# Retention and two gated products on one core: the first block's second group becomes the last group of the first product

## The chip, the core and the metric

One Trainium2 chip, one of its cores. The metric is device time in microseconds (us) for one execution of the whole program, the median of several runs. In the text PE is TensorE, DVE is VectorE, ACT is ScalarE, POOL is GpSimd and SP is SyncE, which issues the transfers. All arithmetic is fp32, and every matmul operand is a pair of fp32r values, a high and a low piece.

## What is computed

```python
# retention: B, H, S, D = 8, 8, 576, 64
scores = scale * np.matmul(q, k.transpose(0, 1, 3, 2))
Dmat = np.where(rel >= 0, gamma[:, None, None] ** rel[None, :, :], 0.0)
x = np.matmul(scores * Dmat[None], v)          # 4608 tokens x 512 features
# first product and its gate, d_ff = 2048
h = x @ w_in
g = h * np.cos(h)
x = g @ w_out
# second product, d_ff = 768
h = np.maximum(np.maximum(x @ w1, x @ w2), x @ w3)
out = h @ w_out2
```

## The kernel before, in words

The 4608 tokens are nine blocks of 512 columns (`NBLK`). Every large product is made by a Strassen-like scheme with seven products instead of eight: `P_A11, P_S1, P_A12, P_S2, P_S4, P_S3, P_A22` is the order within one group. An operand of a product is a tile `x_x{block}_{product}` with a high piece (ACT, L395) and a low piece (DVE, L399); names in the program's order carry the product's number (0 is A11, 3 is S1, 1 is A12, 4 is S2, 6 is S4, 5 is S3, 2 is A22). A weight pair `w_wi{i}` holds the seven products of two column blocks of `w_in`. It is made from the raw weights: two loads (`first_load`), then `widen` (ACT, L191), `join` (DVE, L196 and L197), `total` (POOL, L203), the four sums (DVE, L210 to L213) and the high and low pieces (ACT; DVE, L236 and L232). `lead_in` spreads these over steps by a table of eleven numbers.

The program's order is written by hand. A step (`tick`) ends behind each of PE's products; `at(n, fn)` puts work at the n-th step from now, and each engine executes its instructions in that order. The first 17 steps (`LEAD`) hold the attention of units 0 to 7, that is of blocks 0 and 1 (four units a block, two heads each): `att_scores` (PE, L600), `att_mask` (DVE, L609), `att_products` and `att_out` (PE, L631, L667, L679), `att_decay` (DVE, L695). Then come the groups of the first half of `x @ w_in`, stage A: for each block j two groups, `a{j}_0` with weight pairs `wi0` and `wi1` and `a{j}_1` with `wi2` and `wi3`. A group is seven steps, but the last product (A22) is made in the midst of the next group, so the very first group has six. `group_in` copies or adds the results (ACT L469; DVE L475), and `gate_half` spreads the gate (ACT L526 and L536, DVE L530 and L539) and its store. Between the products stand the attention units of the later blocks (`start_of(n)`, one each 11/3 steps), the building of the operands of block j (`build_in`, due at step 14 j, its differences L391 on POOL except for the last block), their stores to HBM (L792) and, once a block, the making of a further weight pair (`background`). Behind stage A come `in_unit` (the other half of `x @ w_in`, with operands `y` loaded back from HBM by `load_operands`), the product with `w_out`, and the second product; nothing of these is changed but the line numbers.

```python
for i, n in ((2, 10), (3, 13)):          # raw weights of pairs wi2, wi3
at(13, lambda: lead_in(2, 0, nc.vector, nc.vector, SPREAD))
at(16, lambda: lead_in(3, 0, nc.vector, nc.vector, SPREAD))
SPREAD = (0, 1, 2, 1, 2, 3, 5, 4, 5, 6, 7)
```

With this table the first low pieces of `wi3` (for A11, A12 and A22) stand at step 21, those for S1 and S2 at step 23; `a0_1` begins at step 23 and its S1 at step 24.

Of the kernel before, what the change touches and what calls it, by code (L numbers as in the profile page):

```python
# [106 lines left out]
def retention_ffn(ctx: ExitStack, tc: tile.TileContext, att, w_in, w_out, w123, w_out2, cst, out):  # L107
# [19 lines left out]
    def f32(t):  # L127
        return t.bitcast(F32)
# [20 lines left out]
    def at(n, fn, turn=LATER):  # L149
        agenda.setdefault(slot[0] + n, [[], [], [], []])[turn].append(fn)  # L150
# [646 lines left out]
    def block_of(j):  # L797
        return quarters_of.setdefault(j, {"name": f"x{j}", "n": NB})
# [8 lines left out]
    for i, n in ((2, 10), (3, 13)):  # L807
        for p in range(2):
            at(n + p, lambda i=i, p=p: first_load(i, p))
    for k, n in enumerate((NLEAD, NLEAD + 1)):  # L810
        at(13 + 3 * k, lambda n=n: att_load(n))
        at(16 + 3 * k, lambda n=n: att_scale(n))
# [5 lines left out]
    at(13, lambda: lead_in(2, 0, nc.vector, nc.vector, SPREAD))  # L818
    at(16, lambda: lead_in(3, 0, nc.vector, nc.vector, SPREAD))
# [5 lines left out]
    def start_of(n):  # L825
        return 3 + (11 * (n - NLEAD)) // 3
# [6 lines left out]
    for j in range(1, NBLK):  # L833
        build_in(block_of(j), per * j, (-11, -4, -3, -1), (-10, -8, -3, -1, 1, 1, 4), xsd[j], nc.vector if j == NBLK - 1 else nc.gpsimd)
    back = [(k, i) for k, n in (("wi", 4), ("wo", 0)) for i in range(n, 8)]
    back += [("b", i) for i in (0, 1, 2, 4, 3, 5, 6, 7, 8)] + [("o", i) for i in range(3)]
    for j in range(NBLK - 2):
        at(per * j + 1, lambda: background(*back.pop(0), True, 3))
    endA = per * NBLK
    for i, n in enumerate((-29, -22, -15, -8)):  # L840
        more = 0
        take_split("wi", 4 + i, endA + n - 2, endA + n + 4, *(endA + n + 5 + more + m for m in (0, 1, 2, 3)))

# [26 lines left out]

    def gate_half(g, half):
        j, k = g["at"]
        q = slice(2 * half, 2 * half + 2)
        dst = gqp[(j - 1) // 2][k][:, q, (j - 1) % 2] if j else gqs[k][:, q]
        steps = {NBLK - 1: (0, 2, 4, 6), NBLK - 2: (0, 1, 3, 4)}.get(j, range(4))
        gate(g[f"s{half}"], f"{g['name']}_{half}", dst, 0 if half else 3, steps)
# [197 lines left out]
    for j in range(NBLK):  # L1074
        for k in range(2):
            group_in(
                [weights["wi", 2 * k + p] for p in range(2)],
                quarters_of[j],
                f"a{j}_{k}",
                gate_half,  # L1080
                (j, k),
                scale=INV2PI,
                seeded=sums_bank,
            )
# [556 lines left out]
```

## Time and profile before

| | |
|---|---|
| median of 3 runs | 1397.74 us (1394.49 to 1398.34) |
| the profiled execution: its time, its span | 1396.51 us, 1394.7 us |
| PE busy | 1363.3 us, 98% of the span |
| DVE busy | 1129.4 us, 81% |
| ACT, POOL busy | 799.0 us (57%), 230.0 us (16%) |
| HBM read, written | 194.28 MB, 137.89 MB |

The profiled execution's own time and its span differ by 1.8 us, which lie around the span. A busy share is a mean over the whole program; what a wait costs is read from the stretch in which it stands. In the timelines a row gives the start in the span, the duration, the engine, the line, the operation with its tiles, the count, and in brackets the idle time before it with what ended it.

### The profile page before, as it was taken

How to read it: one execution, taken by the hardware profiler on the slowest of the kernel's cores; microseconds unless marked ns; L12 is line 12 of the kernel's file. 1: busy time of each engine (PE TensorE's matmuls, PEld its weight loads, DVE VectorE, ACT ScalarE, POOL GpSimd, SP SyncE). 2: the span in 40 equal slices, each digit the busy share in tenths (PEclk: the TensorE clock that was granted, in tenths of full speed). 3: DMA queues.
4: the chain of work that ended last, by engine and by line, in shares of the span. 5: the costliest groups of instructions: out<-in, count | busy, mean ns of one | idle time of the engine just before them, and what ended most of it. 6: DMA issues, size and time to landing. Idle time of an engine off the chain costs nothing.

```text
span 1394.7 us, 22899 instructions
## 1 busy us (share of the span) xinstructions
PE 1363.3 (98%) x8794; PEld 1175.4 (84%) x8794; DVE 1129.4 (81%) x1471; ACT 799.0 (57%) x1238; POOL 230.0 (16%) x259
## 2 busy tenths in 40 slices
PE   7899999999999999999999999999999999999998
PEld 5799999998888887888988888889878888888887
DVE  8988878989687789989879989577777567868884
ACT  6565565568677876666456556444544434444553
POOL 4455555730110000000011110100100000000000
PEclk9999999999999999999999999999999999999999
DMA  9679899988999975664577997343434476255633
GB/s 387 249 286 333 332 343 311 340 314 318 357 349 339 358 286 211 242 226 173 178 258 207 309 255 209 100 154 114 174 134 159 166 273 252 88 180 155 224 106 121
DMA packets 113085, 333.67 MB, mean 239 GB/s; under 512 B 9936, under 2 KB 18256, under 8 KB 107344
## 3 DMA queue, kind: packets, MB, share of 16 engines
q1 hardware_dynamic: 110096, 322.77, 63.9%
q0 software_dynamic: 2880, 9.44, 3.7%
q8 instruction: 69, 1.13, 0.3%
q14 instruction: 40, 0.33, 0.1%
HBM read 194.28 MB, written 137.89 MB: 238 GB/s over the span
## 4 chain that ended last, share of the span: by engine, by line
PE 55%; DMA 5%; DVE 3%; ACT 1%; issue 1%; SPq 0%; ACTq 0%; DVEq 0%
PE d_e L444 12%; PE d_g L976 11%; PE b_g L976 6%; PE b_e L444 6%; PE d_u L1506 5%; PE a_g L976 3%; PE a_e L444 3%; PE b_u L1506 2%; PE d_b L422 2%; PE a_u L1506 1%; DMA mqp<-ext 1%; PE b_b L422 1%; PE d_gs L976 1%; DMA gqp<-s_a 1%; DMA ar_b<-w 1%
## 5 line engine op out<-in xcount | busy, mean ns | idle before, releaser
L976 PE MATMUL d_g<-h_g,w_wo 128*128 128x512 f32 x512 | 157.9, 390 | 0.5 <-ACT o_g L999 0.5
L444 PE MATMUL in<-y,w_wi 128*128 128x512 f32 x672 | 153.0, 389 | 0.0
L444 PEld LDWEIGHTS in<-y,w_wi 128*128 128x128 f32 x672 | 125.9, 188 | 26.5 <-ACT s_a L1112 0.4
L943 DVE TENSOR_TENSOR l_g<-q_g,h_g 128x1024 fp32r<-128x1024 f32 x96 | 116.7, 1229 | 13.9 <-ACT h_g L936 9.5
L469 ACT ACTIVATE ext<-d_e 128x512 f32<-128x512 f32 x72 | 43.1, 599 | 143.1 <-PE d_e L444 143.1
L422 PE MATMUL d_a<-x_x,w_wi 128*128 128x256 f32 x864 | 117.3, 288 | 7.1 <-DVE w_wi L236 4.8
L936 ACT CAST h_g<-q_g 128x1024 fp32r<-128x1024 f32 x96 | 99.0, 1052 | 35.3 <-DVE q_g L927 22.9
L422 PEld LDWEIGHTS d_a<-x_x,w_wi 128*128 128x128 f32 x864 | 107.7, 192 | 12.3 <-DVE w_wi L236 5.0
L976 PEld LDWEIGHTS d_g<-h_g,w_wo 128*128 128x128 f32 x512 | 95.9, 188 | 20.6 <-ACT o_g L999 0.9
L539 DVE SCALAR_TENSOR_TENSOR s_a<-t_a,s_a 128x1024 f32<-128x1024 f32 x68 | 94.1, 1385 | 12.0 <-ACT t_a L536 12.0
L976 PE MATMUL d_g<-l_g,w_wo 128*128 128x512 f32 x256 | 99.8, 390 | 0.2 <-DVE l_g L943 0.2
L530 DVE SCALAR_TENSOR_TENSOR t_a<-s_a,t_a 128x1024 f32<-128x1024 f32 x68 | 88.5, 1303 | 14.2 <-ACT t_a L526 14.2
L526 ACT ACTIVATE t_a<-s_a 128x1024 int32<-128x1024 f32 x68 | 71.9, 1058 | 21.5 <-DVE s_a L1115 15.3
L536 ACT ACTIVATE t_a<-t_a 128x1024 f32<-128x1024 f32 x68 | 72.0, 1059 | 20.5 <-DVE t_a L530 20.2
L444 PE MATMUL d_e<-h_e,w_b 128*128 128x512 f32 x304 | 81.4, 390 | 0.8 <-DVE ext L473 0.8
L976 PE MATMUL b_g<-h_g,w_wo 128*128 128x512 f32 x256 | 79.2, 390 | 1.5 <-ACT h_g L936 1.5
L473 DVE TENSOR_TENSOR ext<-ext,b_e 128x512 f32<-128x512 f32 x36 | 24.7, 686 | 59.4 <-PE b_e L444 51.7
L444 PEld LDWEIGHTS d_e<-h_e,w_b 128*128 128x128 f32 x304 | 56.9, 188 | 12.9 <-DVE ext L473 1.2
L422 PE MATMUL b_a<-x_x,w_wi 128*128 128x256 f32 x432 | 60.6, 290 | 0.9 <-DVE x_x L399 0.9
L976 PEld LDWEIGHTS b_g<-h_g,w_wo 128*128 128x128 f32 x256 | 47.8, 188 | 12.1 <-ACT h_g L936 2.4
L422 PEld LDWEIGHTS b_a<-x_x,w_wi 128*128 128x128 f32 x432 | 55.3, 195 | 3.2 <-DVE x_x L399 1.1
L976 PEld LDWEIGHTS d_g<-l_g,w_wo 128*128 128x128 f32 x256 | 48.1, 188 | 11.0 <-DVE l_g L943 1.0
(371 smaller groups left out, 3322.4 us busy)
## 6 DMA issues: line engine op xcount, KB each, us to landing
u<-att SPq DMA_DIRECT2D x36, 1028.0 KB, 8.3
gqp<-s_a SPq DMA_DIRECT2D x64, 512.0 KB, 6.8
q_g<-gqp SPq DMA_DIRECT2D x64, 512.0 KB, 7.0
xsp<-x_x SPq DMA_DIRECT2D x56, 512.0 KB, 7.5
y<-xsp SPq DMA_DIRECT2D x56, 512.0 KB, 8.8
mqp<-ext SPq DMA_DIRECT2D x24, 512.0 KB, 4.1
st_b<-p_b SPq DMA_DIRECT2D x21, 512.0 KB, 6.4
w_b<-st_b SPq DMA_DIRECT2D x5, 1792.0 KB, 12.8
```

The source lines that it names most:

```text
L422: nc.tensor.matmul(h[:, p * HB : (p + 1) * HB], a, b, start=first and p == 0 and i == 0, stop=i == len(terms) - 1, skip_group_check=True,)
L444: nc.tensor.matmul(dst, a, b, start=first and i == 0, stop=i == len(terms) - 1, skip_group_check=True)
L469: nc.scalar.activation(dst, b[:, :n], AF.Copy, scale=scale)
L473: nc.vector.tensor_tensor(out=dst, in0=dst, in1=b[:, :n], op=ALU.add)
L526: nc.scalar.activation(st["t"], s, AF.Copy, bias=0.25)
L530: nc.vector.scalar_tensor_tensor(out=r, in0=s, scalar=MOST_TURNS, in1=st["t"], op0=ALU.min, op1=ALU.subtract)
L536: nc.scalar.activation(r, r, AF.Sin, scale=TURN, bias=HALF_PI)
L539: nc.vector.scalar_tensor_tensor(out=s, in0=f32(st["t"]), scalar=-1.0, in1=s, op0=ALU.max, op1=ALU.mult)
L936: nc.scalar.copy(h, ts[i][q])
L943: nc.vector.tensor_tensor(out=lo, in0=t, in1=f32(h), op=ALU.subtract)
L976: nc.tensor.matmul(to, a, v[:, p].rearrange("p (b n) -> p b n", b=2) if half and n == 2 else v[:, :, r], start=first and k == 0 and p == 0 ...
L1506: nc.tensor.matmul(dst, a, v, start=first and p == 0 and i == 0 and (wide or mt == 0), stop=p == 2 and i == 2, skip_group_check=True,)
```

## The change

The order of the groups becomes `a0_0, a1_0, a1_1, a2_0, ..., a8_1, a0_1` (`GROUPS`). The group `a0_1` comes last; its seven operand tiles are loaded from HBM (`load_again`, from the copy `xs0` that was stored for a later stage anyway) at the seven steps from 13 before the end of stage A. Weight pairs `wi2` and `wi3` are first needed by `a1_1`; their loads stand seven steps later and their making six. The operands of block 1 are due seven steps earlier, with a table of their own, and so are those of the later blocks. The attention units from 8 on start at once instead of three steps on, one each 7/2 steps, and the loads of units 8 and 9 stand two steps earlier. The background work of a block stands five steps later. The gates of the last three groups are spread, instead of the last two.

```diff
--- before.py
+++ after.py
@@ -804,42 +804,52 @@
     SPREAD = (0, 1, 2, 1, 2, 3, 5, 4, 5, 6, 7)
     for n in range(4, NLEAD):
         at(2 * n - 5, lambda n=n: att_load(n))
-    for i, n in ((2, 10), (3, 13)):
+    for i, n in ((2, 17), (3, 20)):
         for p in range(2):
             at(n + p, lambda i=i, p=p: first_load(i, p))
     for k, n in enumerate((NLEAD, NLEAD + 1)):
-        at(13 + 3 * k, lambda n=n: att_load(n))
-        at(16 + 3 * k, lambda n=n: att_scale(n))
+        at(11 + 3 * k, lambda n=n: att_load(n))
+        at(15 + 3 * k, lambda n=n: att_scale(n))
     lead_in(0, 0, nc.vector, nc.vector, FIRST)
     at(3, claim)
     at(4, lambda: lead_in(1, 0, nc.vector, nc.vector, SECOND))
     for n in range(NLEAD):
         att_unit(n, 2 * n + 1)
-    at(13, lambda: lead_in(2, 0, nc.vector, nc.vector, SPREAD))
-    at(16, lambda: lead_in(3, 0, nc.vector, nc.vector, SPREAD))
+    at(19, lambda: lead_in(2, 0, nc.vector, nc.vector, SPREAD))
+    at(22, lambda: lead_in(3, 0, nc.vector, nc.vector, SPREAD))
     build_in(block_of(0), 0, (10, 14, 15, 16), (10, 12, 14, 16, 17, 18, 19), xsd[0], nc.vector)
     for _ in range(LEAD):
         tick()
 
 
     def start_of(n):
-        return 3 + (11 * (n - NLEAD)) // 3
+        return (7 * (n - NLEAD)) // 2
 
     for n in range(NLEAD, NUNIT):
         if n > NLEAD + 1:
             at(max(0, start_of(n) - 4), lambda n=n: att_load(n))
         att_unit(n, start_of(n))
     per = 14
-    for j in range(1, NBLK):
-        build_in(block_of(j), per * j, (-11, -4, -3, -1), (-10, -8, -3, -1, 1, 1, 4), xsd[j], nc.vector if j == NBLK - 1 else nc.gpsimd)
+    build_in(block_of(1), 7, (-7, -3, -2, -1), (-6, -5, -2, -1, 0, 1, 4), xsd[1], nc.gpsimd)
+    for j in range(2, NBLK):
+        build_in(block_of(j), per * j - 7, (-11, -4, -3, -1), (-10, -8, -3, -1, 1, 1, 4), xsd[j], nc.vector if j == NBLK - 1 else nc.gpsimd)
     back = [(k, i) for k, n in (("wi", 4), ("wo", 0)) for i in range(n, 8)]
     back += [("b", i) for i in (0, 1, 2, 4, 3, 5, 6, 7, 8)] + [("o", i) for i in range(3)]
     for j in range(NBLK - 2):
-        at(per * j + 1, lambda: background(*back.pop(0), True, 3))
+        at(per * j + 6, lambda: background(*back.pop(0), True, 3))
     endA = per * NBLK
     for i, n in enumerate((-29, -22, -15, -8)):
         more = 0
         take_split("wi", 4 + i, endA + n - 2, endA + n + 4, *(endA + n + 5 + more + m for m in (0, 1, 2, 3)))
+
+    again = {}
+
+    def load_again(product):
+        x = again[product] = x4(f"again_{product}", [2, NB], F32R)
+        nc.sync.dma_start(out=f32(x), in_=xss[:, product])
+
+    for r, product in enumerate((P_A11, P_S1, P_A12, P_S2, P_S4, P_S3, P_A22)):
+        at(endA - 13 + r, lambda product=product: load_again(product))
 
     IN_ORDER = (P_A11, P_A12, P_S2, P_S1, P_S3, P_S4, P_A22)
     later_x = {}
@@ -868,11 +878,14 @@
         n = endA + (10, 38, 66, 90)[i]
         take_split("wo", i, n, n + 5, n + 6, n + 7, n + 9, n + 10)
 
+    GROUPS = [(0, 0), *((j, k) for j in range(1, NBLK) for k in range(2)), (0, 1)]
+
     def gate_half(g, half):
         j, k = g["at"]
         q = slice(2 * half, 2 * half + 2)
         dst = gqp[(j - 1) // 2][k][:, q, (j - 1) % 2] if j else gqs[k][:, q]
-        steps = {NBLK - 1: (0, 2, 4, 6), NBLK - 2: (0, 1, 3, 4)}.get(j, range(4))
+        place = GROUPS.index((j, k)) - len(GROUPS)
+        steps = (0, 2, 4, 6) if place >= -3 else (0, 1, 3, 4) if place >= -5 else range(4)
         gate(g[f"s{half}"], f"{g['name']}_{half}", dst, 0 if half else 3, steps)
 
 
@@ -1071,17 +1084,18 @@
             wo_units.append(wo_unit(m, half, base_of[half, m]))
         return base
 
-    for j in range(NBLK):
-        for k in range(2):
-            group_in(
-                [weights["wi", 2 * k + p] for p in range(2)],
-                quarters_of[j],
-                f"a{j}_{k}",
-                gate_half,
-                (j, k),
-                scale=INV2PI,
-                seeded=sums_bank,
-            )
+    for j, k in GROUPS:
+        group_in(
+            [weights["wi", 2 * k + p] for p in range(2)],
+            again if (j, k) == (0, 1) else quarters_of[j],
+            f"a{j}_{k}",
+            gate_half,
+            (j, k),
+            scale=INV2PI,
+            seeded=sums_bank,
+        )
+        if k or not j:
+            quarters_of.pop(j, None)
 
     in_banks = []
```

**PE, between the first group and the next.** `a0_0` is the first group, `x_x1_...` are operands of block 1, `w_wi3` is the last weight pair. Before:

```order
L422 MATMUL b_a0_0_643<-x_x0_6_634,w_wi0_180 128x256 x6
L422 MATMUL b_a0_0_643<-x_x0_6_634,w_wi1_303 128x256 x6
L422 MATMUL d_a0_0_614<-x_x0_5_691,w_wi0_180 128x256 x6
L422 MATMUL d_a0_0_614<-x_x0_5_691,w_wi1_303 128x256 x6
L422 MATMUL d_a0_1_841<-x_x0_0_410,w_wi2_636 128x256 x6
L422 MATMUL d_a0_1_841<-x_x0_0_410,w_wi3_787 128x256 x6
```

Now the group `a1_0` follows, with the weights that are there already:

```order
L422 MATMUL d_a0_0_591<-x_x0_5_678,w_wi0_180 128x256 x6
L422 MATMUL d_a0_0_591<-x_x0_5_678,w_wi1_303 128x256 x6
L631 MATMUL kv9_815<-u2_1_511 64x64 x6
L667 MATMUL po8_822<-u2_0_420 64x128 x8
L679 MATMUL po8_822<-u2_0_420,spare_131 64x128 x2
L679 MATMUL po8_822<-u2_0_420 64x128 x4
L422 MATMUL d_a1_0_849<-x_x1_0_682,w_wi0_180 128x256 x6
L422 MATMUL d_a1_0_849<-x_x1_0_682,w_wi1_303 128x256 x6
L422 MATMUL b_a1_0_884<-x_x1_3_706,w_wi0_180 128x256 x6
L422 MATMUL b_a1_0_884<-x_x1_3_706,w_wi1_303 128x256 x6
```

and `wi2`, `wi3` are read first by `a1_1`, behind it:

```order
L422 MATMUL d_a1_0_849<-x_x1_5_967,w_wi0_180 128x256 x6
L422 MATMUL d_a1_0_849<-x_x1_5_967,w_wi1_303 128x256 x6
L631 MATMUL kv11_1077<-u2_3_869 64x64 x6
L667 MATMUL po10_1084<-u2_2_767 64x128 x8
L679 MATMUL po10_1084<-u2_2_767,spare_131 64x128 x2
L679 MATMUL po10_1084<-u2_2_767 64x128 x4
L422 MATMUL d_a1_1_1109<-x_x1_0_682,w_wi2_875 128x256 x6
L422 MATMUL d_a1_1_1109<-x_x1_0_682,w_wi3_995 128x256 x6
L422 MATMUL b_a1_1_1135<-x_x1_3_706,w_wi2_875 128x256 x6
L422 MATMUL b_a1_1_1135<-x_x1_3_706,w_wi3_995 128x256 x6
```

Between the end of S3 of `a0_0` and the first matmul with `w_wi3` stood six matmuls; now a whole group, two scores and three attention visits stand there.

**DVE, ahead of the last low pieces of `wi3`.** The row `w_wi3...<-s_wi3` makes the low pieces for S1, S2 and S3, S4. Before:

```order
L236 TENSOR_TENSOR w_wi3_787<-fa_wi3_700,w_wi3_787 128x2x256
L232 SCALAR_TENSOR_TENSOR w_wi3_787<-fa_wi3_700,w_wi3_787 128x256
L609 TENSOR_TENSOR u2_0_483<-sc8_0_770,cs_132 128x512
L609 TENSOR_TENSOR u2_0_483<-sc8_1_771,cs_132 128x512
L475 SCALAR_TENSOR_TENSOR s1_a0_0_656<-d_a0_0_614,s1_a0_0_656 128x512
L399 TENSOR_TENSOR x_x1_0_818<-k1_x1_557,x_x1_0_818 128x512
L196 TENSOR_SCALAR ar_wi4_704<-ar_wi4_704 128x512
L197 SCALAR_TENSOR_TENSOR ar_wi4_704<-ar_wi4_704 128x512
L236 TENSOR_TENSOR w_wi3_787<-s_wi3_809,w_wi3_787 128x2x256 x2
```

Now the same piece of the order, which holds the gate of `a0_0` and the additions of `a1_0`:

```order
L236 TENSOR_TENSOR w_wi3_995<-fa_wi3_921,w_wi3_995 128x2x256
L232 SCALAR_TENSOR_TENSOR w_wi3_995<-fa_wi3_921,w_wi3_995 128x256
L196 TENSOR_SCALAR ar_wi4_882<-ar_wi4_882 128x512
L197 SCALAR_TENSOR_TENSOR ar_wi4_882<-ar_wi4_882 128x512
L475 SCALAR_TENSOR_TENSOR s0_a1_0_862<-b_a1_0_884,s0_a1_0_862 128x512
L609 TENSOR_TENSOR u2_3_869<-sc11_0_1013,cs_132 128x512
L609 TENSOR_TENSOR u2_3_869<-sc11_1_1014,cs_132 128x512
L530 SCALAR_TENSOR_TENSOR t_a0_0_1_1038<-s1_a0_0_640,t_a0_0_1_1038 128x1024
L475 SCALAR_TENSOR_TENSOR s1_a1_0_897<-d_a1_0_849,s1_a1_0_897 128x512
L399 TENSOR_TENSOR x_x1_2_1056<-tb_x1_795,x_x1_2_1056 128x512
L399 TENSOR_TENSOR x_x2_0_1058<-k1_x2_864,x_x2_0_1058 128x512
L236 TENSOR_TENSOR w_wi3_995<-s_wi3_1029,w_wi3_995 128x2x256 x2
```

and the rows with which the way there begins, from the addition behind S4 of `a0_0` (L475):

```order
L475 SCALAR_TENSOR_TENSOR s0_a0_0_604<-b_a0_0_627,s0_a0_0_604 128x512
L695 SCALAR_TENSOR_TENSOR k2_x1_697<-po7_731,cs_132 128x64
L695 SCALAR_TENSOR_TENSOR k2_x1_697<-po7_731,cs_132 128x192
L695 SCALAR_TENSOR_TENSOR k2_x1_697<-po7_731,cs_132 128x256
L609 TENSOR_TENSOR u2_1_511<-sc9_0_750,cs_132 128x512
L609 TENSOR_TENSOR u2_1_511<-sc9_1_751,cs_132 128x512
L196 TENSOR_SCALAR t_wi2_708<-t_wi2_708 128x512
L197 SCALAR_TENSOR_TENSOR raw_wi2_1_670<-raw_wi2_1_670,t_wi2_708 128x512
L475 SCALAR_TENSOR_TENSOR s1_a0_0_640<-d_a0_0_591,s1_a0_0_640 128x512
L695 SCALAR_TENSOR_TENSOR k1_x2_864<-po8_822,cs_132 128x128 x2
L695 SCALAR_TENSOR_TENSOR k1_x2_864<-po8_822,cs_132 128x256
L399 TENSOR_TENSOR x_x1_1_843<-k2_x1_697,x_x1_1_843 128x512
```

What moved: the making of `wi2` and `wi3` left the time of block 0's operands and now stands among the operands of block 1, three decays, three masks and the gate of `a0_0`.

**SP, at the end of stage A.** `xsp3<-x_x8...` are stores of the last block's operands, `gqp...<-s` stores of a gate, `y0` the operands of the next stage. Before:

```order
L792 DMA xsp3_75<-x_x8_1_4112 128x2x512
L857 DMA y0_00_4198<-xsp0_72 128x1024
L857 DMA y0_01_4199<-xsp0_72 128x1024
L792 DMA xsp3_75<-x_x8_4_4153 128x2x512
L545 DMA gqp3_0_92<-s1_a7_0_3787 128x2x512
L792 DMA xsp3_75<-x_x8_6_4194 128x2x512
L792 DMA xsp3_75<-x_x8_5_4196 128x2x512
L349 DMA fa_wi7_4261<-wf_wi7_122 128x1024
L857 DMA y0_10_4281<-xsp0_72 128x1024
L857 DMA y0_11_4282<-xsp0_72 128x1024
L545 DMA gqp3_1_93<-s0_a7_1_3995 128x2x512
L792 DMA xsp3_75<-x_x8_2_4256 128x2x512
```

Now the last store of block 8's operands stands ahead, and the loads `again` stand among those of `y0`:

```order
L792 DMA xsp3_75<-x_x8_2_4129 128x2x512
L849 DMA again_0_4207<-xs0_71 128x1024
L867 DMA y0_00_4209<-xsp0_72 128x1024
L867 DMA y0_01_4210<-xsp0_72 128x1024
L849 DMA again_3_4226<-xs0_71 128x1024
L545 DMA gqp3_1_93<-s1_a7_1_3891 128x2x512
L849 DMA again_1_4248<-xs0_71 128x1024
L349 DMA fa_wi7_4268<-wf_wi7_122 128x1024
L849 DMA again_4_4270<-xs0_71 128x1024
L849 DMA again_6_4288<-xs0_71 128x1024
L867 DMA y0_10_4290<-xsp0_72 128x1024
L867 DMA y0_11_4291<-xsp0_72 128x1024
```

## Rows read from the trace of the kernel before

**Rows 1.** Stretches: us; PE, PEld, DVE, ACT, POOL busy; PEclk, DMA share, GB/s

```profile
50.00:60.00 10.00, 3.44 (x25) 2.93 (x24) 9.93 (x21) 4.55 (x10) 4.11 (x4) 0.96 0.57 210
60.00:70.00 10.00, 10.00 (x88) 9.07 (x89) 7.86 (x14) 3.40 (x6) 2.83 (x4) 0.70 0.47 153
```

**Rows 2.** Timeline of PE, from the first group to the second score behind it

```profile
37.23 1.69 PE L422 MATMUL d_a<-x_x,w_wi 128*128 128x256 f32 x12
38.76 1.60 PE L422 MATMUL b_a<-x_x,w_wi 128*128 128x256 f32 x12
...
53.08 1.93 PE L422 MATMUL d_a<-x_x,w_wi 128*128 128x256 f32 x14 [1.77 <-DVE x_x L399]
59.80 1.65 PE L422 MATMUL d_a<-x_x,w_wi 128*128 128x256 f32 x6 [4.79 <-DVE w_wi L236]
61.38 2.08 PE L600 MATMUL sc<-u 64*128 64x128 f32 x16
63.38 2.84 PE L422 MATMUL b_a<-x_x,w_wi 128*128 128x256 f32 x12
...
67.58 0.57 PE L631 MATMUL kv<-u 128*64 128x64 f32 x12
...
69.75 3.13 PE L422 MATMUL d_a<-x_x,w_wi 128*128 128x256 f32 x24
72.81 1.16 PE L600 MATMUL sc<-u 64*128 64x128 f32 x16
```

**Rows 3.** Timeline of DVE, ahead of the last pieces of the fourth weight pair

```profile
37.47 0.84 DVE L391 TENSOR_TENSOR ta_x<-k_x,k_x 128x512 f32<-128x512 f32 x1
...
53.67 2.49 DVE L236 TENSOR_TENSOR w_wi<-s_wi,w_wi 128x512 fp32r<-128x512 f32 x2
...
56.69 0.99 DVE L695 SCALAR_TENSOR_TENSOR k_x<-po,cs 128x64 f32<-128x64 f32 x3
57.60 0.41 DVE L210 TENSOR_TENSOR s_wi<-fa_wi 128x256 f32<-128x256 f32 x1
...
59.06 0.68 DVE L236 TENSOR_TENSOR w_wi<-fa_wi,w_wi 128x512 fp32r<-128x512 f32 x1
...
59.99 1.28 DVE L609 TENSOR_TENSOR u<-sc,cs 128x512 f32<-128x512 f32 x2
61.19 0.68 DVE L475 SCALAR_TENSOR_TENSOR s_a<-d_a,s_a 128x512 f32<-128x512 f32 x1
61.79 0.68 DVE L399 TENSOR_TENSOR x_x<-k_x,x_x 128x512 fp32r<-128x512 f32 x1
62.39 0.42 DVE L196 TENSOR_SCALAR ar_wi<-ar_wi 128x512 uint32<-128x512 uint32 x1
...
63.45 1.28 DVE L236 TENSOR_TENSOR w_wi<-s_wi,w_wi 128x512 fp32r<-128x512 f32 x2
64.66 1.28 DVE L609 TENSOR_TENSOR u<-sc,cs 128x512 f32<-128x512 f32 x2
```

**Rows 4.** Timeline of DVE near the end of stage A, one operation of a gate

```profile
318.00 1.22 DVE L530 SCALAR_TENSOR_TENSOR t_a<-s_a,t_a 128x1024 f32<-128x1024 f32 x1
```

**Rows 5.** Timeline of POOL, one of each kind that the change moves

```profile
51.44 1.04 POOL L203 TENSOR_TENSOR fa_wi<-raw_wi 128x512 uint32<-128x512 uint32 x1 [2.70 <-DVE raw_wi L197]
52.43 0.77 POOL L653 TENSOR_TENSOR u<-u 128x64 f32<-128x64 f32 x1
...
70.59 1.30 POOL L391 TENSOR_TENSOR tb_x<-k_x,ta_x 128x512 f32<-128x512 f32 x1
```

**Rows 6.** Stretch table, the time in which DVE was behind

```profile
35.50:64.10 28.60, 22.04 (x259) 20.28 (x256) 28.36 (x55) 16.23 (x33) 13.85 (x17) 0.91 0.64 254
```

**Rows 7.** What PE waited for from 320 to 345 us

```profile
PE b_a L422 <- DVE x_x L399: 0.9, 1, 0.9
PE d_a L422 <- DVE x_x L399: 0.4, 1, 0.4
```

**Rows 8.** Issues from 318 to 342 us, the last number us to landing

```profile
y<-xsp SPq DMA_DIRECT2D x8, 512.0 KB, 8.8
```

## The prediction

> **What bounds the kernel now.** The page gives PE 98% of the span, so whatever this change brings must come out of the few places where PE waits, or out of new ones. I first read what PE waited for, then the timelines of PE and DVE at these places, then the stretch tables. The change touches stage A alone, and there PE waits twice.
>
> Early, in the first groups: PE is idle 1.77 us ahead of 53.08, for a low piece of an operand, and 4.79 us ahead of 59.80, for the first low piece of `wi3` [rows 2]. Behind these waits it runs slower: the score at 61.38 takes 2.08 us where a later one takes 1.16, S1 at 63.38 takes 2.84 where such a product takes 1.60, and the six matmuls at 59.80 take 1.65, where half a product is about 0.8 [rows 2]. These three are 0.9 + 1.2 + 0.8 = 2.9 us longer. The granted clock of that stretch says why: 0.70 on average from 60 to 70 us [rows 1], a mix of the levels 2.4 and 1.2 GHz, after a stretch in which PE was busy 3.44 of 10 us. So the early loss is 1.77 + 4.79 + 2.9 = **9.5 us**. DVE is what PE waits for: it is busy 9.93 of 10 us from 50 to 60 [rows 1], and 28.36 of 28.6 us from 35.5 to 64.1 [rows 6]. PE is the bound over the whole program, DVE in this stretch.
>
> Late, at the last block, PE waits 0.9 + 0.4 = 1.3 us for operands of block 8 [rows 7].
>
> **The change, part by part.** *What it takes away.* The making of `wi2` and `wi3` leaves the DVE queue ahead of block 0's operands, so these are early and the first wait goes. The second goes from its place too: no matmul of the first group reads those weights any more. If nothing else became late, 9.5 us were gained. What is late next is the same weights, one group on.
>
> *When PE wants `wi3` now.* I count from the end of S4 of `a0_0`, since there DVE stands at the addition (L475) that waits for S4: what the order puts on DVE ahead of it is block 0's and block 1's first operands, without the weights, and in the old order DVE got through these and more by then. From there PE has, up to the second half of S1 of `a1_1`, which is the first to read the second low pieces of `wi3`: nine products at 1.53 us (37.23 to 38.76), half a product at 0.8, two scores at 1.16, and three attention visits at 2.17 (67.58 to 69.75) [rows 2]. That is 13.8 + 0.8 + 2.3 + 6.5 = **23.4 us**.
>
> *What DVE has to do until then*, from start to start [rows 3]: four additions L475 at 0.60 (2.4), three decays at 0.91 (2.7), three masks at 1.20 (3.6), four joins at 1.06, three for `wi2` and `wi3` and one of the background work (4.2), six low pieces of operands at 0.60 (3.6), the sums of two weight pairs at 1.46 (2.9), their first low pieces at 0.93 (1.9), the second ones, 1.21 and the first 0.6 of the last (1.8), and three operations of the gate at 1.2 [rows 4] (3.6): **26.7 us**. So even with no disturbance DVE comes 3.3 us late. The old order had the same race over two and a half products in place of nine and a half, with a DVE that was behind already. The longer way gives PE more to do, but it also puts ahead of the weights what stood behind them before: the gate of `a0_0`, masks, decays and operands of block 1.
>
> *The disturbance.* DVE's operations on two SBUF tensors take longer while POOL works: the pair at 53.67 takes 2.49 us, at 63.45 only 1.28 [rows 3]. From 37.47 to 53.67 ten DVE instructions are stretched so, by 4.5 us together, while POOL is busy 13.85 us [rows 6]: a third of POOL's time. In the new stretch POOL has four differences at 1.30, four totals at 1.04 and three small pairs at about 0.77 [rows 5], and two scalings of V, which I take like a total: 5.2 + 4.2 + 2.3 + 2.1 = 13.8 us. A third of it is **4.6 us**; the bounds are nothing, and two thirds (9.2), if POOL's time hides only beside the third of DVE's time that reads PSUM (additions, decays, masks: 8.7 of 26.7 us). I take the third, since rows 6 are the same engines in the same kind of work.
>
> The page "SBUF — State Buffer" of the Trainium skill, section "Who interferes with whom", speaks against the change here: a DVE instruction with two SBUF inputs and a GpSimd instruction that reads SBUF exclude each other for a whole instruction. The trace agrees in kind, the 2.49 us beside the 1.28; read strictly, the rule gives the 9.2 in place of the 4.6, and a sum 4.6 us higher.
>
> *The sum of the early part.* 26.7 + 4.6 - 23.4 = 7.9 us of waiting, most of it at A11 and S1 of `a1_1`, close together as now, so the same slow stretch behind it: 2.9 us. The loss is 10.8 in place of 9.5: **+1.3 us**. Cost bounds: waiting 3.3 to 12.5, slow clock 0 to 3.
>
> *The loads.* The raw weights leave SP's queue ahead of unit 8's and unit 9's loads; those come earlier, and their scores too. I cost both at nothing: fewer bytes stand ahead of them. If that cover went, the score of unit 8 would hold PE by what its load lacks. The raw loads themselves have DVE's backlog as cover.
>
> *The rest of stage A* keeps its ratio: four units a block instead of 3.8, the same operands and gates, and each block's last decay as far ahead of its products as block 7's now, where PE doesn't wait. I put it at nothing; so I do the wider spreading of one more gate, which nobody waits for before the product with `w_out`. For block 8 there is one step more (1.5 us) between its last decay and its first product, but also one more join (1.06) in front: the 1.3 us [rows 7] shrink to about 0.9, **-0.4 us**.
>
> *The last group* reads seven loads of 512 KB, each six to eight steps ahead of its use, six steps being 9.2 us at 1.53 [rows 2]. Loads in that part take 8.8 us to land [rows 8], and SP issues in order: behind the first two of them stand a store that waits for DVE's gate (L539) and the loads of `y0`. So some land late, between 0 and 4 us in all (a load that lands a step or two later than those rows holds its product by that step, and the following ones are then late no further). I take **+0.8 us**; the loads of `y0`, which they delay, are due thirteen steps on and cost nothing.
>
> Sum: 1.3 - 0.4 + 0.8 = **+1.7 us** on the profiled execution's 1396.5: 1398.2. The median shown, 1397.74, is 1.2 above that execution, so a median run should come to about 1399.4; I say **1399**, no difference that a measurement of this kernel can tell (that takes about 0.3%, 4.2 us).
>
> **The rivals.**
> *DVE keeps up (faster).* POOL's work falls beside masks, decays and additions, the wait is the bare 3.3 us or less, and the clock doesn't fall. Then 9.5 - 3.3 + 0.4 = 6.6 us are gained, 1391. For it: a third of DVE's work on this way reads PSUM, and 3.3 us is half of what PE waits now. Against it: by rows 6 POOL's work has a price in just this mix.
> *POOL shuts DVE out (slower).* The mechanism is the shared reading of SBUF; its place is the stretch from S4 of `a0_0` to S1 of `a1_1`; it decides if more than half of POOL's 13.8 us lies on DVE's path. With 9.2 us the wait is 26.7 + 9.2 - 23.4 = 12.5, the loss 15.4 in place of 9.5: 5.9 - 0.4 + 0.8 = 6.3 us more, 1404. For it: all differences of block 1 now stand beside the making of both weight pairs. Against it: a third only is what rows 6 show. The skill's rule above is this rival.
> *The reload is late (slower).* If the queue is full when the first `again` load is issued, each of the last group's products waits, 4 us in place of 0.8: 1402 to 1403. For it: rows 8, 8.8 us against 9.2 of lead. Against it: the last block's stores stand earlier now, and the first loads find a shorter queue.
> *The change doesn't do what it says*, that is, `wi3` is wanted no later against DVE's clock: that is half true by the count above, and is in the forecast.
>
> **How the numbers follow.** The forecast has 0.5, DVE keeping up 0.2, POOL 0.16, the reload 0.14. The range reaches from 1390 (the first rival, less a little) to 1405 (the second with a bit of the third); about 2 in 10 lie outside. Faster by over 0.3% is the first rival, 0.2. Slower by over 0.3% is the second and nearly all of the third, 0.28. The rest is 0.52.
>
> **What would show it.** In the profile of the changed kernel the waits at 53 and 59 us are gone, PE runs on to about 75 us, and there, at `a1_1`, stands a wait of 5 to 10 us for L236, with a granted clock below 1 behind it. DVE is busy nearly all of 52 to 83 us, with L399 and L236 at up to twice their length. In the last group waits for `again` are below 2 us. I am wrong if PE doesn't wait at `a1_1` (then faster), if it waits over 11 us there or for `again` over 3 us (then slower), or if waits stand in the blocks between, where I see none.

## The result and the profile after

The changed kernel takes **1406.54 us** (median of 4 runs, 1405.71 to 1407.45) where the kernel before took 1396.35 in the same comparison: a ratio of **1.0073**, 95% interval 1.0054 to 1.0092. It is slower, and outside the range that was forecast. Its profiled execution took 1405.78 us with a span of 1404.0, the one of before 1396.51 with 1394.7. All of the difference is made in stage A: the first matmul of the next stage starts at 349.0 us, before at 339.3, and behind it the two traces keep their distance to within 0.5 us.

What PE waited for in the changed kernel, 30 to 350 us (engine, tile and line <- what it waited for: us in total, times, longest):

```profile
PE b_a L422 <- DVE w_wi L236: 5.3, 1, 5.3
PE b_a L422 <- DMA again<-xs: 3.1, 1, 3.1
PE sc L600 <- DVE u L609: 1.6, 1, 1.6
PE b_a L422 <- DVE x_x L399: 1.2, 2, 0.9
PE d_a L422 <- DMA again<-xs: 1.1, 2, 0.6
PE d_a L422 <- DVE w_wi L236: 0.9, 1, 0.9
PE d_a L422 <- DVE x_x L399: 0.5, 1, 0.5
PE sums L422 <- DVE x_x L399: 0.4, 1, 0.4
```

**Early.** The waits of before at 53 and 59 us [rows 2] are gone and stand 16 to 26 us later. Timeline of PE in the changed kernel, the rows with a wait and those behind them:

```profile
69.00 1.16 PE L600 MATMUL sc<-u 64*128 64x128 f32 x14 [1.55 <-DVE u L609]
...
71.07 2.08 PE L422 MATMUL b_a<-x_x,w_wi 128*128 128x256 f32 x8 [0.24 <-DVE x_x L399]
72.94 2.27 PE L422 MATMUL d_a<-x_x,w_wi 128*128 128x256 f32 x12
...
79.21 0.98 PE L422 MATMUL d_a<-x_x,w_wi 128*128 128x256 f32 x6 [0.92 <-DVE w_wi L236]
...
86.19 1.65 PE L422 MATMUL b_a<-x_x,w_wi 128*128 128x256 f32 x6 [5.29 <-DVE w_wi L236]
87.77 2.08 PE L600 MATMUL sc<-u 64*128 64x128 f32 x16
89.78 2.41 PE L422 MATMUL sums<-x_x,w_wi 128*128 128x256 f32 x12
```

The four waits are 1.55 + 0.24 + 0.92 + 5.29 = 8.0 us. The rows at 71.07, 72.94, 86.19, 87.77 and 89.78 are 0.9 + 0.7 + 0.85 + 0.9 + 0.7 = 4.0 us longer than such rows are elsewhere (1.22 for eight matmuls, 1.60 and 1.70 for twelve, 0.8 for six, 1.16 for a score). The granted clock of these stretches, ahead of the last two columns, is 0.83 and 0.73, between the two levels of 1.2 and 2.4 GHz, against 0.70 from 60 to 70 us before [rows 1]:

```profile
70.00:80.00 10.00, 8.84 (x78) 7.86 (x77) 9.93 (x17) 7.05 (x12) 2.13 (x2) 0.83 0.40 159
80.00:90.00 10.00, 4.71 (x31) 4.05 (x30) 9.50 (x16) 3.63 (x5) 3.76 (x5) 0.73 0.74 266
```

So the early loss is 12.0 us, 2.5 more than the 9.5 of before.

**Late.** Timeline of PE in the last group, which reads the reloaded operands:

```profile
332.53 1.67 PE L422 MATMUL d_a<-again,w_wi 128*128 128x256 f32 x12
337.31 2.90 PE L422 MATMUL b_a<-again,w_wi 128*128 128x256 f32 x12 [3.11 <-DMA again<-xs]
340.01 1.86 PE L422 MATMUL sums<-again,w_wi 128*128 128x256 f32 x12
342.33 1.70 PE L422 MATMUL d_a<-again,w_wi 128*128 128x256 f32 x12 [0.46 <-DMA again<-xs]
...
347.52 1.67 PE L422 MATMUL d_a<-again,w_wi 128*128 128x256 f32 x12 [0.61 <-DMA again<-xs]
349.03 2.91 PE L444 MATMUL in<-y,w_wi 128*128 128x512 f32 x12
```

From A11 of this group at 332.53 to the end of stage A at 349.03 pass 16.5 us. Seven such products without a wait take 10.1 (seen in the first experiment), so the reload costs **6.4 us**: 4.2 of waiting, the rest mostly in the two slow rows behind it (2.90 and 1.86 where 1.60 is usual; the granted clock is 0.72 from 335 to 340 us). SP's own timeline shows how the loads came to be late, and the table of issues (325 to 345 us; last number: median us from issue to landing) how long they took:

```profile
326.03 0.36 SPq L792 DMA_DIRECT2D xsp<-x_x  x1
326.44 0.46 SPq L849 DMA_DIRECT2D again<-xs  x1
327.00 1.30 SPq L867 DMA_DIRECT2D y<-xsp  x2
328.35 0.42 SPq L849 DMA_DIRECT2D again<-xs  x1
```

```profile
again<-xs SPq DMA_DIRECT2D x7, 512.0 KB, 10.1
```

S1's load is the one at 328.35; ahead of it SP issued a store that had waited for DVE's low piece, the load for A11 and a pair of `y0`. PE was ready for S1 at 334.0 (332.53 and one product), and the load landed at 337.2, 8.8 us behind its issue.

**The sum.** Early +2.5, reload +6.4, the waits of block 8 now 0.95 + 0.45 + 0.37 = 1.8 in place of 1.3 [rows 7] (+0.4), and the first group started 0.4 us later (37.67 against 37.23): 9.7 of the 9.8 us. The last of these terms cannot be put down to the change: in profiles of kernels whose edits lie behind that place the first group starts anywhere from 37.34 (e2_gate6) to 41.03 us (e11_y_late). From the first group's first matmul to that of the next stage, which is called the length of stage A below, pass 311.4 us, before 302.0.

### The profile page after: what moved, and what is told of

It reads as the page before. It is cut to its first block, busy times and chain, and to the rows that moved or that the text cites. A ratio compares the mean times of both kernels' runs of the same rounds, so it can differ in the third digit from the quotient of the medians.

```text
span 1404.0 us, 22915 instructions
## 1 busy us (share of the span) xinstructions
PE 1366.2 (97%) x8794; PEld 1177.6 (84%) x8794; DVE 1133.3 (81%) x1471; ACT 799.9 (57%) x1238; POOL 222.0 (16%) x259
## 3 DMA queue, kind: packets, MB, share of 16 engines
q1 hardware_dynamic: 111104, 326.44, 64.5%
## 4 chain that ended last, share of the span: by engine, by line
PE 65%; DMA 6%; DVE 4%; ACT 1%; issue 1%; SPq 0%; ACTq 0%; DVEq 0%
PE d_e L444 13%; PE d_g L989 11%; PE in L444 8%; PE b_e L444 6%; PE b_g L989 6%; PE d_u L1520 5%; PE a_e L444 3%; PE a_g L989 3%; PE b_u L1520 2%; PE d_b L422 2%; DMA again<-xs 1%; PE a_u L1520 1%; DMA mqp<-ext 1%; PE b_b L422 1%; PE d_gs L989 1%
## 5 line engine op out<-in xcount | busy, mean ns | idle before, releaser
L422 PE MATMUL d_a<-x_x,w_wi 128*128 128x256 f32 x816 | 109.8, 287 | 1.4 <-DVE w_wi L236 0.9
L422 PEld LDWEIGHTS d_a<-x_x,w_wi 128*128 128x128 f32 x816 | 101.7, 192 | 5.4 <-issue 2.1
L530 DVE SCALAR_TENSOR_TENSOR t_a<-s_a,t_a 128x1024 f32<-128x1024 f32 x68 | 83.9, 1235 | 12.7 <-ACT t_a L526 12.0
```

The source lines that it names most:

```text
L422: nc.tensor.matmul(h[:, p * HB : (p + 1) * HB], a, b, start=first and p == 0 and i == 0, stop=i == len(terms) - 1, skip_group_check=True,)
L530: nc.vector.scalar_tensor_tensor(out=r, in0=s, scalar=MOST_TURNS, in1=st["t"], op0=ALU.min, op1=ALU.subtract)
```

## The experiments

Each edit is made on the changed kernel, unless it says otherwise; ratios are to the kernel before, which ran beside them (medians 1396.5 to 1397.4).

| label | edit | median us | ratio, 95% interval |
|---|---|---|---|
| e1_again7 | reload 7 steps earlier | 1400.50 | 1.0035, 1.0023 to 1.0046 |
| e6_actq | reload on ACT's queue | 1403.82 | 1.0053, 1.0040 to 1.0066 |
| e11_y_late | loads of `y0` 5 steps later | 1402.92 | 1.0035, 1.0022 to 1.0047 |
| e2_gate6 | gate of `a0_0` 6 steps later | 1401.27 | 1.0037, 1.0024 to 1.0049 |
| e3_pool | block 1's differences on DVE | 1404.42 | 1.0057, 1.0042 to 1.0071 |
| e7_again_gate | e1 and e2 | 1396.94 | 0.9996, 0.9986 to 1.0006 |
| e8_low3 | e7, low pieces of `wi3` earlier | 1394.01 | 0.9980, 0.9969 to 0.9991 |
| e9_mask_first | e8, masks ahead of `wi2`'s sums | 1393.71 | 0.9977, 0.9965 to 0.9989 |
| e10_low3_pool | e8 and e3 | 1395.28 | 0.9982, 0.9970 to 0.9993 |
| e12_all | e9, e3, background 3 steps later | 1398.06 | 1.0002, 0.9990 to 1.0014 |
| e13_background | e10, background 3 steps later | 1397.69 | 1.0001, 0.9990 to 1.0012 |
| e14_mask_pool | e9 and e3 | 1392.36 | 0.9968, 0.9956 to 0.9980 |

### The reload: late because of what?

```diff
-        at(endA - 13 + r, lambda product=product: load_again(product))
+        at(endA - 20 + r, lambda product=product: load_again(product))
```

> The seven loads of the last group's operands are issued seven steps earlier; nothing else is changed. Theory (the reload is the large term: PE waited 3.11 + 0.46 + 0.61 us for it in the changed kernel, and about 1.7 us more went in the slower matmuls behind): these waits go, the stretch from 325 to 350 us is shorter by 5 to 6 us, and the time is about 1400.5, a ratio to the kernel before of 1.003. Rival (the wait only marks where the queue to the DMA engines is full, and the loads of y0 or the last blocks' stores take the place of `again`): other loads land late by as much, and the time stays within 1.5 us of the changed kernel's 1406.5, a ratio of 1.007.

Measured 1400.50, 6.0 us less, as the theory had it. All seven products of the last group run on without a wait, from 332.46 to 342.54, and the clock stays up (e1_again7: first and last row of the last group with the next stage behind it, and the same stretch as above):

```profile
332.46 1.60 PE L422 MATMUL d_a<-again,w_wi 128*128 128x256 f32 x12
342.54 2.91 PE L444 MATMUL in<-y,w_wi 128*128 128x512 f32 x12
```

```profile
335.00:340.00 5.00, 5.00 (x44) 5.00 (x43) 5.00 (x6) 4.24 (x8) 0.00 (x0) 1.00 1.03 410
```

The DMA engines are as full as before (1.03), and nothing else comes late. That leaves open whether the loads were late because SP issued them late or because the DMA engines were full.

```diff
-        nc.sync.dma_start(out=f32(x), in_=xss[:, product])
+        nc.scalar.dma_start(out=f32(x), in_=xss[:, product])
```

> The seven loads of the last group's operands are issued at the same steps by ScalarE's queue in place of SyncE's; nothing else is changed. In the changed kernel SP issued the first of them at 326.44 us, after it had been held to 326.03 by a store of block 8 that waits for DVE, and it landed some 10 us later. Theory A (they are late since SP issued them late): the issue of the first moves to about 323 to 324 us, they land 2 to 3 us earlier, PE's waits for them fall from 4.2 to about 1.5 us or less. Theory B (they are late since the DMA engines are full, busy 1.02 to 1.04 from 335 to 350 us): issued earlier or not, they land at the same time to within 1 us, and PE waits 3.5 to 4.5 us.

As an experiment on theory A this is a miss: ACT was held by its own work too and issued the first load at 326.31, not at 323, so theory A was not put to the test. What it shows is that issuing them from another engine's queue does not bring these loads in time: landing took 9.0 us, and now A11 had to wait.

```profile
334.57 1.92 PE L422 MATMUL d_a<-again,w_wi 128*128 128x256 f32 x12 [2.63 <-DMA again<-xs]
```

The waits were 3.4 us in place of 4.2; of the 2.7 us by which the median is lower, this trace shows 1.2 in stage A, and the rest stays open. The Trainium skill has this in "DMA: Bandwidth & Descriptors", section "Issuing engines are not separate DMA queues": whichever engine starts a DMA, it runs on the same 16 DMA engines, and several issuers save only the time of issuing. This trace agrees (10.1 and 9.0 us).

```diff
-        load_operands(m, endA + 28 * m + 1)
+        load_operands(m, endA + 28 * m + 1 + (5 if m == 0 else 0))
```

> As the kernel changed as given, but the loads of y0 (pairs of 512 KB for the next part) come five steps later; the loads of the last group's operands keep their steps. In the changed kernel S1's load of `again` was issued at 328.35 us, right behind a pair of y0, and landed at 337.3. Theory (the loads are late because the transfers ahead of them fill the DMA engines): without that pair it lands some 2.6 us earlier (two transfers of 512 KB at about 400 GB/s), PE's waits for `again` fall from 4.2 to about 1.5 us, the slower matmuls behind them (1.7 us) mostly go, and the time falls by 2.5 to 4.5 us, to 1402 to 1404, if y0 itself is still in time. Rival (issue and landing take their 9 to 10 us whatever is queued; the loads are issued too late): the waits stay at 3.5 to 4.2 us, the time within 1.5 us of 1406.5. Second rival: y0 is late in turn and PE waits at the first matmuls of the next part.

Measured 1402.92, 3.6 us less, in the range of the theory. The loads of `again` keep their steps and land in 6.8 us in place of 10.1; of the 4.2 us of waiting 0.8 is left:

```profile
again<-xs SPq DMA_DIRECT2D x7, 512.0 KB, 6.8
```

```profile
342.01 1.69 PE L422 MATMUL d_a<-again,w_wi 128*128 128x256 f32 x12 [0.83 <-DMA again<-xs]
```

`y0` itself was not late. S1's load was issued some 7 us ahead of its product in place of 5.6, since SP had no pair of `y0` to issue before it, and it landed in 6.3 us in place of 8.8; the larger part is in the landing. So the transfers queued ahead are the cause that can be shown. SP's hold to 326.03 makes the lead short as well; that was not tried alone. (The profiled execution of this kernel started its first group 3.4 us later than the changed kernel's, far ahead of the edit; its stage A is 306.8 us long in place of 311.4.)

### The early part: order on DVE's queue

```diff
-        gate(g[f"s{half}"], f"{g['name']}_{half}", dst, 0 if half else 3, steps)
+        gate(g[f"s{half}"], f"{g['name']}_{half}", dst, (0 if half else 3) + (6 if (j, k) == (0, 0) else 0), steps)
```

> The two halves of the gate of a0_0 come six steps later; nothing else is changed. That moves three DVE operations of 1.2 us (both of the first half, one of the second) from ahead of the second low pieces of wi3 to behind them. Theory (PE at a1_1 waits for DVE's queue alone, 8.0 us in the changed kernel): the waits of a0_0 to a1_1 come to 4.4 us, 3.6 less, and the slower matmuls behind them lose up to 2 us less, so the time is 3 to 5.5 us below the changed kernel's, 1401 to 1403.5, a ratio of 1.003 to 1.005. Rival (DVE is held back by what it waits for, PE's own products among it, not by its own length of work): the waits stay at 7 to 8 us and the time at 1406.

Measured 1401.27, 5.3 us less, as the theory had it. PE waits only twice from 60 to 95 us, 5.4 us where 4.4 were expected:

```profile
PE b_a L422 <- DVE w_wi L236: 3.8, 1, 3.8
PE sc L600 <- DVE u L609: 1.6, 1, 1.6
```

The second low pieces of `wi3` were done at 83.2 in place of 86.7 (the changed kernel's row first, then e2_gate6's):

```profile
85.46 1.28 DVE L236 TENSOR_TENSOR w_wi<-s_wi,w_wi 128x512 fp32r<-128x512 f32 x2
```

```profile
82.00 1.28 DVE L236 TENSOR_TENSOR w_wi<-s_wi,w_wi 128x512 fp32r<-128x512 f32 x2
```

So what stands ahead on DVE's queue sets this wait. The trace accounts for 2.6 us less of early waiting, 0.8 less in the slow rows behind it and 0.3 at the reload; the rest of the 5.3 is not assigned.

```diff
-    build_in(block_of(1), 7, (-7, -3, -2, -1), (-6, -5, -2, -1, 0, 1, 4), xsd[1], nc.gpsimd)
+    build_in(block_of(1), 7, (-7, -3, -2, -1), (-6, -5, -2, -1, 0, 1, 4), xsd[1], nc.vector)
```

> The four differences of block 1's operands are made by DVE in place of POOL; nothing else is changed. DVE gets four operations of 0.6 us more (2.4 us), POOL loses four of 1.3 us (5.2 us), which lie beside the making of both weight pairs. Theory of the forecast (a third of POOL's time lands on DVE): DVE gains 1.7 us and loses 2.4, the wait at a1_1 grows by 0.7 us, the time by 0 to 1.5 us. Rival (POOL shuts DVE out for two thirds of its time): DVE gains 3.5 us and loses 2.4, the wait shrinks by 1.1 us. If the low pieces and weight sums beside these differences keep their stretched lengths (L399 and L236 at about twice 0.6 and 1.2 us), the stretch comes from the totals (L203) and the scalings instead.

Measured 1404.42, 2.1 us less. The intervals of the two kernels overlap, but the traces point the same way: stage A is 309.1 us long in place of 311.4. So the forecast's theory (a loss) is not borne out for these operations. The wait for the masks is gone; PE, earlier by it, waits longer at the next places, 7.7 us in all in place of 8.0. Most of the gain lies in the slower matmuls (2.7 us in place of 4.0) and in the reload (0.6). Three of the four differences lay in the stretch from 52 to 87 us. There POOL's busy time (the fifth of the busy columns) falls from 11.39 + 7.46 = 18.9 to 5.79 + 7.47 = 13.3. The changed kernel:

```profile
52.00:67.00 15.00, 15.00 (x173) 13.65 (x171) 14.39 (x22) 9.59 (x19) 11.39 (x11) 1.00 0.91 350
67.00:87.00 20.00, 12.00 (x102) 10.58 (x102) 19.90 (x33) 10.91 (x18) 7.46 (x8) 0.85 0.54 200
```

and e3_pool:

```profile
52.00:67.00 15.00, 14.89 (x170) 13.48 (x170) 14.40 (x28) 10.53 (x20) 5.79 (x7) 1.00 0.97 375
67.00:87.00 20.00, 12.30 (x113) 10.50 (x114) 19.93 (x32) 10.48 (x18) 7.47 (x8) 0.88 0.53 208
```

The sum of what DVE's rows there are longer than their like without POOL falls from 7.0 to 3.8 us. So on average 7.0 / 18.9 = 0.37 us of DVE per us of POOL, but for the work taken away 3.2 / 5.6 = 0.57. Only 4.3 of these 5.6 us are the three differences; most of the rest is a total that now ran before 52 us, and by the differences alone the price is 3.2 / 4.3 = 0.74. The DMA engines were no less busy without the differences (0.97 and 0.53 against 0.91 and 0.54, the column before the last), so what went is due to POOL and not to the transfers. The low pieces of `wi3` came 1.4 us earlier, which is 3.2 less the 1.8 that DVE took on.

### Both terms at once, and how far the order carries

The reload seven steps earlier and the gate six later:

> Both single edits at once: the reload seven steps earlier (alone it took the time from 1406.5 to 1400.5 us) and the gate of a0_0 six steps later (alone to 1401.3). Theory (the loss of the change is two separate terms, one early on DVE's queue and one late in the reload): they add, 6.0 + 5.3 = 11.3 us below the changed kernel, 1395.2 us, between 1393.5 and 1397, a ratio to the kernel before of 0.998 to 1.000. Rival (the early part only shifts in time what the late part then waits for, so that one wait swallows a part of the other's gain): 1398 to 1400, a ratio of 1.001 to 1.003.

Measured 1396.94, at the upper end of what was expected; by the ratios, which take out that the kernel before ran 0.7 us slower here, the two gains would give 0.9999, and 0.9996 was measured. The terms add, and the change as repaired is level with the kernel before.

```diff
-    at(22, lambda: lead_in(3, 0, nc.vector, nc.vector, SPREAD))
+    at(22, lambda: lead_in(3, 0, nc.vector, nc.vector, (0, 1, 2, 1, 2, 3, 4, 3, 4, 4, 5)))
```

> As the kernel with both edits, and the last low pieces of wi3 (L236 of the sums) come two steps earlier, right behind their sums. On DVE's queue they pass one join, two additions, a pair of masks and two operand low pieces, 4.7 to 5.2 us by the trace of the kernel with the later gate, where PE still waited 3.8 us for them and then ran some 1.7 us longer at the lower clock. Theory (what counts is only which DVE work stands ahead of the piece PE wants; DVE as a whole is not too slow): the wait of 3.8 us goes and the slow matmuls with it, 4 to 5.5 us less than the kernel with both edits, about 1390 us, a ratio of 0.994 to 0.997. Rival (DVE is short of time in total, so the work that was overtaken is late next): a new wait for L475 or L609 of 2 us or more stands between 84 and 95 us, and the gain is below 2 us.

Measured 1394.01, 2.9 us less: between the two. The wait for L236 is gone, and a new one of 2.6 us stands at 78 us, not where the rival looked for it: PE waits for ACT to copy a bank out (L458).

```profile
78.23 2.48 PE L422 MATMUL d_a<-x_x,w_wi 128*128 128x256 f32 x12 [2.64 <-ACT s_a L458]
```

ACT's timeline in the same kernel shows why. The high pieces (L227) wait 5.25 us for the sums that DVE makes last, at 75.9, and two background operations and then the copy stand behind them in ACT's order:

```profile
75.27 1.29 ACT L227 CAST w_wi<-s_wi 128x512 fp32r<-128x512 f32 x2 [5.25 <-DVE s_wi L211]
76.46 0.67 ACT L191 ACTIVATE ar_wi<-ar_wi 128x512 f32<-128x512 f32 x1
77.03 0.66 ACT L192 ACTIVATE ar_wi<-ar_wi 128x512 uint32<-128x512 uint32 x1
77.58 0.59 ACT L458 ACTIVATE s_a<-d_a 128x512 f32<-128x512 f32 x1
```

```diff
-    at(19, lambda: lead_in(2, 0, nc.vector, nc.vector, SPREAD))
+    at(19, lambda: lead_in(2, 0, nc.vector, nc.vector, (0, 1, 2, 1, 2, 3, 6, 4, 6, 6, 7)))
```

> As the kernel with the earlier low pieces of wi3, and the sums and first low pieces of wi2 come one step later, so that a pair of masks (L609) and an operand's low piece (L399) pass them on DVE's queue by 2.4 us. In the kernels so far PE waited 1.56 us at a score for these masks (near 69 us), and the score and the product behind it ran some 1.6 us longer. Theory: this wait and the slow matmuls go, 1.5 to 3 us less than without the edit. Rival (wi2 and wi3 are late next): the wait turns up at S1 or A11 of a1_1 for L236, and the gain is below 1 us.

Measured 1393.71, which cannot be told from e8_low3. The rival was right in its number (a gain below 1 us) but not in its place: the wait for the masks is gone, and the lateness turns up through ACT at two copies:

```profile
PE d_a L422 <- ACT s_a L469: 2.2, 1, 2.2
PE d_a L422 <- ACT s_a L458: 1.2, 1, 1.2
```

e8_low3 with block 1's differences on DVE:

> As the kernel with the earlier low pieces of wi3, and block 1's differences made by DVE in place of POOL. With the kernel changed as given this edit alone brought 2.1 us: DVE took on 1.8 us in the stretch and lost 3.2 us of stretched operations. If the remaining early wait is DVE's length (theory), it brings 1 to 2 us here too; if what is left waits for something else (the score's bank, a load), nothing, within 0.5 us.

Measured 1395.28: no gain that could be told. In its trace the wait for the masks is gone, but the 2.6 us at L458 stay; stage A is 297.5 us long there against 298.9, the gain that the theory had, but in one execution of each. Inconclusive by itself.

```diff
-        at(per * j + 6, lambda: background(*back.pop(0), True, 3))
+        at(per * j + 6 + (3 if j == 0 else 0), lambda: background(*back.pop(0), True, 3))
```

> All edits together (the reload seven steps earlier, the gate of a0_0 six later, the low pieces of wi3 two earlier, the masks ahead of wi2's sums, block 1's differences on DVE), and the first background weight three steps later, so that its two ACT operations (1.2 us) and its join no longer stand between the high pieces of wi3 and the copy (L458) that PE waits for. Theory (what is left early is DVE's length and ACT's order behind it): of the 2.2 + 1.2 us that PE waited at d_a with the masks first, POOL's relief takes about 1.4 and the reordering 1.1, so the time is 1 to 3 us below the 1393.7 us of the kernel with the masks first, 1391 to 1392.7, a ratio to the kernel before of 0.996. Rival (DVE is short in total from 52 to 80 us, and each reordering only moves the wait): PE's waits between 60 and 95 us still come to 3 us or more, and the time is within 1 us of 1393.7.

> As the kernel with the earlier low pieces of wi3 and block 1's differences on DVE, and the first background weight three steps later; the masks keep their place behind wi2's sums. There PE waited 2.64 us for the copy L458, which stood on ACT behind the high pieces of wi3 (waiting for DVE's sums) and two background operations. Theory: the background operations are 1.1 to 1.2 us of these 2.64, and the wait falls to about 1.5 us, the time by 1 to 2 us, to about 1393.5. Rival: the copy waits for the sums alone, and nothing changes.

Both are a miss: 1398.06 and 1397.69, 5.7 and 2.4 us slower than the same kernels with the background weight in its place (e14_mask_pool and e10_low3_pool; the intervals of e12_all and e14_mask_pool lie apart, those of e13_background and e10_low3_pool overlap a little, and stage A is 4.2 and 5.8 us longer in the traces). The wait for L458 did fall, to 1.4 and 1.5 us, as expected. But the background work takes its tiles from the buffers that the attention units use. Now SP waits 9.1 us for PE to free a buffer before it may issue the next background load, the store of the background work comes later behind it, SP waits for that store before it may issue an attention load, and PE waits for an attention load issued behind that one. SP and PE in e12_all:

```profile
SPq L185 <- PE po L679: 9.1, 1, 9.1
SPq L566 <- DMA wf_wi<-ar_wi: 3.9, 1, 3.9
```

```profile
122.62 1.16 PE L600 MATMUL sc<-u 64*128 64x128 f32 x16 [3.39 <-DMA u<-att]
```

e9_mask_first with block 1's differences on DVE:

> As the kernel with the masks first (reload, gate, low pieces of wi3, masks), and block 1's differences on DVE; the background weight stays at its old steps, since moving it held an attention load back and cost more than it gave. Theory (each us that DVE gets back from POOL's stretch shortens the 2.2 + 1.2 us that PE still waits at d_a): 0.7 to 1.5 us below the 1393.7 us with the masks first, 1392.2 to 1393, a ratio to the kernel before of 0.996 to 0.9975. Rival (with the masks first POOL's work falls beside other DVE work, and DVE takes on 1.8 us for 1.8 of stretch): within 0.5 us of 1393.7.

Measured **1392.36**, the fastest: below the kernel before by 4.2 us (0.9968, 0.9956 to 0.9980) and below the changed one by 14. From e9_mask_first it is 1.3 us, in the range of the theory, but the two intervals overlap, and stage A is 0.9 us shorter in the traces: this last step is likely, not shown. With both edits, PE's early waits are 3.0 us:

```profile
PE d_a L422 <- ACT s_a L458: 2.5, 1, 2.5
PE d_a L422 <- ACT s_a L469: 0.5, 1, 0.5
```

## Why the prediction was wrong

**The step that failed is the reload: "I take +0.8 us", measured 6.4.** The mechanism was named, as the third rival, and sized wrong in three places. Its lead was counted in steps of 1.53 us from the table (9.2 us), but the last block has no attention work and PE goes by products of 1.44 us there, while SP stood two steps behind the table: the load for A11 was issued at 326.44, where six products ahead of A11 are 323.9, and S1's 5.6 us before PE was ready for it. Its landing was taken from rows 8 (8.8 us), a stretch without these loads; the change itself adds seven transfers of 512 KB to it, and they took 10.1 in the median. And the rival's 4 us, which are the 4.2 us of waiting, left out the slower matmuls behind, 2.2 us, though the same prediction counts such a slow stretch in the early part. "The first loads find a shorter queue", which spoke against the rival, holds for the first load alone: it took 6.0 us, the second 8.8, and all others 10.0 or more. The prediction had named over 3 us of waiting for `again` as a sign of being wrong; it was 4.2. Of the 8.1 us by which the traced loss of 9.8 exceeds the +1.7 of the sum, 5.6 are the reload, 1.2 the early part, 0.8 block 8 and 0.4 the start of the first group.

**The early part was right in mechanism and mostly in place, and in its wait by luck.** 8.0 us of waiting against 7.9, of which 6.2 stood at A11 and S1 of `a1_1`, as was said, and 1.8 ahead of them, at a score and a product of `a1_0`, where the forecast had none. But DVE took 33.6 us from the addition at 52.51 to about 86.1, where the low piece that PE waits for is done (the first of the two in the row at 85.46), not 31.3, and PE's own way to the same place, the wait at 86.19 less the 8.0 us, was 26.0 us from 52.2, not 23.4. DVE's undisturbed work was well counted (33.6 less 7.0 is 26.6; forecast 26.7). The price per us of POOL's time, a third, held on average (0.37), but POOL was busy 18.9 us in the stretch, not 13.8: a total of the background weight (1.04) and a third scaling (2.02) fell into it too, and POOL's own rows were longer there than counted (totals of 1.49 and 1.48 for 1.04). PE was slower mostly since it already waited 1.55 us for masks at 69 us, which the count did not see, and ran at the lower clock behind that. The slow stretch was 4.0 us in place of 2.9. Together +2.5 in place of +1.3.

**The second rival, POOL shutting DVE out**, did not come as a whole: the stretch is 7.0 us, midway between the forecast's 4.6 and the rival's 9.2, but over the 18.9 us that POOL worked this is 0.37, near the forecast's third. For block 1's differences, though, the price was 0.57 to 0.74 by e3_pool, about the rival's two thirds. The Trainium skill's strict rule ("SBUF — State Buffer", section "Who interferes with whom") is by these numbers a bound for the operations that fall on it, not a price for all of POOL's time.

**DVE keeps up**, the faster rival, fails in the change as given: DVE is busy 34.3 of the 35 us from 52 to 87. **The change does what it says.**

**Block 8** was taken at -0.4 and came at +0.4: the two waits of before are as they were (0.95 and 0.45), and one of 0.37 is new; what makes it, no run tests. The rest of stage A, the gates' spreading and the earlier loads cost nothing that the trace shows, as said. The forecast of "no difference" with 0.52 thus failed mainly by the reload: with it repaired (e1_again7) the ratio is 1.0035, a small loss still, and 1400.5 is close to the 1399 that was said.

## What to carry to other kernels

A load's lead is the time from its real issue, as the issuing queue's timeline shows it, to the moment at which the consumer is ready; a step in a table is neither, and the landing time must be that of the queue after the change, its own new transfers included. Where an engine is busy all the time over a stretch, give the first places in its queue to what the bound engine wants next, and look at what the other engines queue behind it: when the wait of L236 was cured, it came back through ACT at L458. A long wait on PE can cost more than its length, where the matmuls behind it run at the lower clock: here 4.0 us on 8.0, and 2.2 on 4.2. Short ones need not: behind the wait of 0.95 us at block 8 the rows have their usual lengths:

```profile
319.92 1.22 PE L422 MATMUL b_a<-x_x,w_wi 128*128 128x256 f32 x8 [0.95 <-DVE x_x L399]
320.98 3.04 PE L422 MATMUL d_a<-x_x,w_wi 128*128 128x256 f32 x24
```

## What the runs showed of the hardware

- With the DMA engines at 1.02 to 1.04 and some 410 GB/s, a load of 512 KB took 10.1 us from issue to landing in the median of seven, without the pair of `y0` ahead 6.8, and on ACT's queue 9.0.
- A DVE shift with one SBUF operand was longer beside POOL as well: L196 took 1.26 us at 59.51 while a total (L203) ran on POOL, and 0.41 at 67.21 while POOL was idle.
- POOL's time had no single price for DVE: 0.37 us per us over the stretch, 0.57 to 0.74 where three differences beside DVE's operations on two SBUF tensors were taken away.
